# 32 bytes in front of the inner activations of two feed-forward layers: their start moves from 96 to 0 modulo 128

## The chip, the core and the metric

The kernel runs on one core of a Trainium2 chip. The metric is the device time of one execution in microseconds (us), as the median of several runs. Three runs of the kernel before took 557.93, 558.11 and 560.37 us.

## What is computed

Soft-capped attention over 2 batches of 12 heads (448 tokens, head size 64) is followed by two feed-forward layers on its 896 x 768 result. Each layer multiplies by a 768 x 2048 matrix, applies an activation, and multiplies by a 2048 x 768 matrix.

```python
def _attn_ref(q, k, v, cap):
    scores = scale * np.matmul(q, k.transpose(0, 1, 3, 2))
    scores = cap * np.tanh(scores / cap)
    scores = scores - np.max(scores, axis=-1, keepdims=True)
    attn = np.exp(scores)
    attn = attn / (np.sum(attn, axis=-1, keepdims=True) + 1e-09)
    return np.matmul(attn, v).astype(np.float32)

x = attn_out.transpose(0, 2, 1, 3).reshape(B * S, H * D)      # 896 x 768
h = x @ moe_w_in        # 768 x 2048
g = np.where(h >= 1, h, np.where(h <= -1, 0.0, (h + 1) ** 2 / 4))
x = g @ moe_w_out       # 2048 x 768
h = x @ moe2_w_in
g = np.maximum(0.01 * h, h)
out = g @ moe2_w_out
```

## The kernel before, in words

**Stages.** The attention runs in six steps of four heads each. Its result is kept transposed in SBUF as `xh` and `xl` (lines 178 and 179): the model's 768 columns lie in 6 chunks of 128 partitions, and the 896 tokens in the free dimension, as two batches of 448. Then follow four stages of matmuls: the first layer in (called in-stage 1 here), the first layer out (out-stage 1), the second layer in (in-stage 2), the second layer out (out-stage 2). An in-stage reads `xh` and `xl` and makes `gh` and `gl`, 16 chunks of 128 partitions by 896 tokens; an out-stage reads `gh` and `gl` and makes the next `xh` and `xl`, or the output.

**High and low parts.** Every float32 operand is split into a part that the reduced format fp32r holds and the rest: `xh` and `xl`, `gh` and `gl`, and for the weights `whi` and `wlo`. A product is made of three matmuls (`products`, lines 241 to 251): `whi` with the high part (line 247), `whi` with the low part (line 248), `wlo` with the high part (line 251). Each loads a 128 x 128 block of weights into the array, which the profile shows as PEld, and streams 448 columns of the activations, which are the moving operand. For a weight chunk the six matmuls come in the order 247, 248 for batch 0, 247, 248 for batch 1, then 251 twice. In-stages and out-stages go through the same six lines, with the same weight buffers.

**Weights.** They arrive as 64-bit numbers, are converted by ACT and DVE (`weights`, lines 194 to 239) and land in four pairs of buffers `whi0`/`wlo0` to `whi3`/`wlo3` (line 192), which all four stages use in turn. A block of weights is 768 columns wide in an in-stage and 512 in an out-stage. `Plan.order` sets one order of issue for all engines ahead of time.

**Where the tiles lie.** The tiles of a pool are laid out one behind the other, and each begins at a multiple of 32 bytes within a partition. The built program has these start addresses:

| tile | bytes per partition | start | start modulo 128 |
|---|---|---|---|
| `xh` | 21504 | 16512 | 0 |
| `xl` | 21504 | 38016 | 0 |
| `whi0` (first of the 8 weight buffers) | 3072 | 78048 | 96 |
| `wlo3` (last of them) | 3072 | 99552 | 96 |
| `gh` | 57344 | 102624 | 96 |
| `gl` | 57344 | 159968 | 96 |
| `a0`, `a1`, `a2` | 3584 each | 217312 on | 96 |

Three one-column tiles (`capb`, `rcap`, `half`) of 32 bytes each stand behind `xl`, which is why everything behind them lies at 96. All steps within these tiles (3584 bytes from chunk to chunk, 1792 from batch to batch, 512 from one 128-column block of weights to the next) are multiples of 128, so a tile's remainder is that of every matmul operand in it. `gh`, `gl` and the three `a` tiles, which hold the activation on its way from PSUM to `gh` and `gl`, are in the pool "layers" (lines 597 to 600). It opens when the first activation of a layer is issued, over the place of the attention's pool, which closes there.

Of the kernel before, what the change touches and what calls it, by code (L numbers as in the profile page):

```python
# [8 lines left out]
F32 = mybir.dt.float32  # L9
# [116 lines left out]
def tile_softcap_attention_ffn_ffn(  # L126
# [23 lines left out]
    NPAIR, P, _, S = qt.shape  # L150
# [443 lines left out]
    with tc.manual_schedule():  # L594
        for _, t in plan.order():
            if t["part"] == "act" and not later:
                st.close()
                pool = ctx.enter_context(tc.tile_pool(name="layers", bufs=1))
                later["g"] = [pool.tile([P, KF, NT], F32R, name=x) for x in ("gh", "gl")]
                later["a"] = [pool.tile([P, B, S], F32, name=f"a{n}") for n in range(3)]  # L600
            t["fn"]()
# [51 lines left out]
```

## Time and profile before

| | before |
|---|---|
| median of three runs | 558.11 us |
| the profiled execution | 558.62 us |
| its span from first to last instruction | 556.8 us |
| PE (matmuls) busy | 549.4 us, 99% of the span |
| PEld (weight loads) busy | 461.4 us, 83% |
| DVE busy | 394.4 us, 71% |
| ACT busy | 265.0 us, 48% |
| attention and its overlap with in-stage 1 | 0 to 91.4 us |
| in-stage 1, undivided part | 91.4 to 204.3 us |
| out-stage 1 | 204.3 to 321.0 us |
| in-stage 2 | 321.0 to 436.3 us |
| out-stage 2 | 436.3 to 552.8 us |

Each matmul's duration overlaps the next one's, and its end is modelled, so a busy share of 99% doesn't tell how fast the matmuls follow each other. That is read from their starts: start to start, in a stretch where the engine waits for nothing. The 1.8 us between the execution's time and its span lie before the first and after the last instruction.

### The profile page before, as it was taken

To read this page: it belongs to the slowest core of one execution; us is meant where nothing else is said; L and a number is where in the kernel's file an instruction comes from. 1 tells how busy PE (TensorE), PEld (TensorE's weight loads), DVE (VectorE), ACT (ScalarE), POOL (GpSimd) and SP (SyncE) were. 2 spreads that over 40 slices of the span, in tenths; PEclk is the share of its full clock that TensorE was granted. 3 is DMA by queue.
4 is the path that set the end of the run, shared out by engine and by line. 5 is a ranking of instruction groups with operands and counts; after the bars stand their busy time and mean duration, and the time that the engine had idled before them with its cause. 6 is when DMAs were issued, how large, how long until landed. Compare 5 with 4: busy or idle time off the path is not lost.

```text
span 556.8 us, 7429 instructions
## 1 busy us (share of the span) xinstructions
PE 549.4 (99%) x2935; PEld 461.4 (83%) x2935; DVE 394.4 (71%) x562; ACT 265.0 (48%) x314; POOL 1.4 (0%) x10
## 2 busy tenths in 40 slices
PE   7999999999999999999999999999999999999997
PEld 4233336999999999999999999999999999999996
DVE  1678787889999988665666579988877755546420
ACT  6999993086667563332223145544444332232210
POOL 0000000000000000000000000000000000000000
PEclk9999999999999999999999999999999999999999
DMA  8555633713332323333324524334222253543400
GB/s 225 163 152 169 199 87 76 215 54 117 114 114 97 112 77 114 114 102 126 105 90 145 171 69 157 116 114 160 86 77 76 52 154 93 150 143 98 125 34 33
DMA packets 25091, 65.06 MB, mean 117 GB/s; under 512 B 5856, under 2 KB 12000, under 8 KB 25056
## 3 DMA queue, kind: packets, MB, share of 16 engines
q1 hardware_dynamic: 24800, 64.24, 37.7%
q8 instruction: 23, 0.38, 0.3%
q10 hardware_dynamic: 224, 0.34, 0.3%
q14 instruction: 12, 0.10, 0.1%
q0 software_dynamic: 32, 0.00, 0.0%
HBM read 61.74 MB, written 2.80 MB: 116 GB/s over the span
## 4 chain that ended last, share of the span: by engine, by line
PE 97%; ACT 2%; issue 0%; DVE 0%
PE d L247 28%; PE d L251 28%; PE d L248 28%; PE d L360 5%; PE d L381 5%; PE d L412 2%; PE d L377 1%; PE d L356 1%; ACT e L365 1%; ACT e L368 1%; PE d L312 1%; ACT a L505 0%; DVE zero L309 0%; DVE half L314 0%
## 5 line engine op out<-in xcount | busy, mean ns | idle before, releaser
L247 PE MATMUL d<-gh,whi 128*128 128x448 f32 x384 | 140.2, 365 | 0.0
L248 PE MATMUL d<-gl,whi 128*128 128x448 f32 x384 | 140.2, 365 | 0.0
L247 PE MATMUL d<-xh,whi 128*128 128x448 f32 x384 | 139.5, 363 | 0.0
L248 PE MATMUL d<-xl,whi 128*128 128x448 f32 x384 | 139.2, 362 | 0.0
L238 ACT CAST whi<-w 128x512 fp32r<-128x512 f32 (+1 forms) x77 | 54.0, 701 | 146.2 <-PE d L248 96.7
L251 PE MATMUL d<-xh,wlo 128*128 128x448 f32 x384 | 111.9, 362 | 0.0
L251 PE MATMUL d<-gh,wlo 128*128 128x448 f32 x384 | 111.7, 365 | 0.0
L172 DVE TENSOR_TENSOR wlo<-w,whi 128x512 fp32r<-128x512 f32 (+1 forms) x80 | 63.5, 794 | 57.5 <-ACT whi L238 57.3
L247 PEld LDWEIGHTS d<-xh,whi 128*128 128x128 f32 x384 | 72.1, 188 | 6.9 <-issue 2.2
L247 PEld LDWEIGHTS d<-gh,whi 128*128 128x128 f32 x384 | 72.1, 188 | 5.7
L251 PEld LDWEIGHTS d<-gh,wlo 128*128 128x128 f32 x384 | 72.1, 188 | 5.7
L248 PEld LDWEIGHTS d<-gl,whi 128*128 128x128 f32 x384 | 72.1, 188 | 5.7
L251 PEld LDWEIGHTS d<-xh,wlo 128*128 128x128 f32 x384 | 72.1, 188 | 4.7
L248 PEld LDWEIGHTS d<-xl,whi 128*128 128x128 f32 x384 | 72.1, 188 | 4.7
L230 ACT ACTIVATE w<-wr 128x512 f32<-128x512 f32 (+1 forms) x77 | 58.5, 760 | 18.7 <-DMA wr<-w1i 8.8
L220 DVE SCALAR_TENSOR_TENSOR w<-wr,w 128x512 int32<-128x512 int32 (+1 forms) x80 | 63.8, 798 | 2.5
L216 DVE SCALAR_TENSOR_TENSOR w<-wr,w 128x512 int32<-128x512 int32 (+1 forms) x80 | 63.8, 798 | 2.4
L471 DVE TENSOR_TENSOR a<-d,a 128x896 f32<-128x896 f32 x32 | 34.7, 1087 | 16.2 <-ACT a L470 15.7
L365 ACT ACTIVATE e<-d,rcap 128x896 f32<-128x896 f32 x42 | 39.6, 1002 | 6.5 <-PE d L360 6.0
L208 DVE TENSOR_SCALAR w<-w 128x512 f32<-128x512 f32 (+1 forms) x80 | 37.9, 473 | 3.8 <-ACT w L230 3.6
L212 DVE TENSOR_SCALAR w<-w 128x512 int32<-128x512 int32 (+1 forms) x80 | 38.4, 480 | 2.7
L368 ACT ACTIVATE e<-e,capb 128x1792 f32<-128x1792 f32 (+1 forms) x18 | 36.7, 2038 | 0.5
(47 smaller groups left out, 320.3 us busy)
## 6 DMA issues: line engine op xcount, KB each, us to landing
wr<-w1o SPq DMA_DIRECT2D x24, 512.0 KB, 3.6
wr<-w2i SPq DMA_DIRECT2D x16, 768.0 KB, 4.3
wr<-w2o SPq DMA_DIRECT2D x24, 512.0 KB, 3.7
wr<-w1i SPq DMA_DIRECT2D x11, 768.0 KB, 4.3
wr<-w1i SPq DMA_DIRECT2D x15, 256.0 KB, 4.9
bc<-rr SPq DMA_DIRECT2D x12, 224.0 KB, 3.9
out<-a SPq DMA_DIRECT2D x12, 224.0 KB, 4.3
v<-vt SPq DMA_DIRECT2D x5, 512.0 KB, 4.6
```

The lines of the kernel that those rows point to most:

```text
L172: nc.vector.tensor_tensor(out=out_, in0=x, in1=f32(hi), op=ALU.subtract)
L208: nc.vector.tensor_scalar(out=f32(w), in0=f32(w), scalar1=W_MIN, scalar2=W_MAX, op0=ALU.max, op1=ALU.min)
L212: nc.vector.tensor_scalar(out=w, in0=w, scalar1=3, scalar2=LOW_30, op0=ALU.logical_shift_left, op1=ALU.bitwise_and)
L216: nc.vector.scalar_tensor_tensor(out=w, in0=r[:, :, 1], scalar=SIGN_AND_TOP, in1=w, op0=ALU.bitwise_and, op1=ALU.bitwise_or)
L220: nc.vector.scalar_tensor_tensor(out=w, in0=r[:, :, 0], scalar=29, in1=w, op0=ALU.logical_shift_right, op1=ALU.bitwise_or)
L230: add("ACT", act(n) + 0.06, lambda: nc.scalar.activation(f32(w), f32(r[:, :, 1]), AF.Abs), R, [W])
L238: add("ACT", act(n), lambda: nc.scalar.copy(h, f32(w)), [W], [H])
L247: nc.tensor.matmul(o[:, b, :S], ch, h[:, f, r], start=first, stop=False)
L248: nc.tensor.matmul(o[:, b, :S], ch, l[:, f, r], start=False, stop=False)
L251: nc.tensor.matmul(o[:, b, :S], cl, h[:, f, r], start=False, stop=last)
L365: add("ACT", act(2 * S, 1), lambda: nc.scalar.activation(e, d[:, :, :S], AF.Tanh, scale=rcap), [("d", s)], [key(j, g)])
L368: lambda: nc.scalar.activation(whole, whole, AF.Exp, scale=capb), [], [key(j, g)])
```

## The change

A tile of 8 float32 per partition (32 bytes) is taken from the pool "layers" ahead of the others. Nothing writes or reads it. `gh` then starts at 102656, `gl` at 160000 and `a0` at 217344, all multiples of 128. The weights, `xh` and `xl` stay where they were, and the last tile ends at 228096. Every engine's instructions stand in the same order as before, with waits on the same engines at the same places.

```diff
             if t["part"] == "act" and not later:
                 st.close()
                 pool = ctx.enter_context(tc.tile_pool(name="layers", bufs=1))
+
+                pool.tile([P, 8], F32, name="pad")
                 later["g"] = [pool.tile([P, KF, NT], F32R, name=x) for x in ("gh", "gl")]
                 later["a"] = [pool.tile([P, B, S], F32, name=f"a{n}") for n in range(3)]
             t["fn"]()
```

## Rows read from the trace of the kernel before

**Rows 1.** The page: engines' busy time, and the granted TensorE clock in 40 slices.
```profile
PE 549.4 (99%) x2935; PEld 461.4 (83%) x2935; DVE 394.4 (71%) x562; ACT 265.0 (48%) x314; POOL 1.4 (0%) x10
PEclk9999999999999999999999999999999999999999
```

**Rows 2.** All waits of PE: engine, line waited for, us in total, times, longest.
```profile
PE d L381 <- ACT e L368: 2.4, 2, 1.4
PE d L312 <- DVE half L314: 1.4, 1, 1.4
```

**Rows 3.** PE's groups by form: line, operands, count, busy us, mean ns, idle before.
```profile
L247 PE MATMUL d<-gh,whi 128*128 128x448 f32 x384 | 140.2, 365 | 0.0
L248 PE MATMUL d<-gl,whi 128*128 128x448 f32 x384 | 140.2, 365 | 0.0
L247 PE MATMUL d<-xh,whi 128*128 128x448 f32 x384 | 139.5, 363 | 0.0
L248 PE MATMUL d<-xl,whi 128*128 128x448 f32 x384 | 139.2, 362 | 0.0
```

**Rows 4.** Timeline, PE, in-stage 2: start us, duration, line, matmul (x2: two merged).
```profile
379.86 0.36 PE L247 MATMUL d<-xh,whi 128*128 128x448 f32 x1
380.06 0.36 PE L248 MATMUL d<-xl,whi 128*128 128x448 f32 x1
...
384.66 0.36 PE L247 MATMUL d<-xh,whi 128*128 128x448 f32 x1
```

**Rows 5.** The same view: the edges of out-stage 1.
```profile
204.29 0.36 PE L247 MATMUL d<-gh,whi 128*128 128x448 f32 x1
...
321.03 0.37 PE L247 MATMUL d<-xh,whi 128*128 128x448 f32 x1
321.23 0.36 PE L248 MATMUL d<-xl,whi 128*128 128x448 f32 x1
321.44 0.37 PE L247 MATMUL d<-xh,whi 128*128 128x448 f32 x1
321.64 0.37 PE L248 MATMUL d<-xl,whi 128*128 128x448 f32 x1
321.85 0.57 PE L251 MATMUL d<-xh,wlo 128*128 128x448 f32 x2
322.26 0.36 PE L247 MATMUL d<-xh,whi 128*128 128x448 f32 x1
```

**Rows 6.** The same view, all engines: first matmul of out-stage 2, and the kernel's end.
```profile
436.26 0.36 PE L247 MATMUL d<-gh,whi 128*128 128x448 f32 x1
...
552.79 0.37 PE L251 MATMUL d<-gh,wlo 128*128 128x448 f32 x1
553.20 0.53 ACT L505 COPY a<-d 128x448 f32<-128x448 f32 x1 [1.90 <-PE d L251]
553.75 0.33 SPq L506 DMA_DIRECT2D out<-a  x1
```

**Rows 7.** Line 251: operation, count: duration in ns, min/median/max, first and last start.
```profile
L251 PE MATMUL d<-xh,wlo x384: 360/362/370, 85.8 to 436.1; 128*128 128x448 f32 x192
L251 PE MATMUL d<-gh,wlo x384: 362/365/369, 205.1 to 552.8; 128*128 128x448 f32 x192
```

**Rows 8.** Busy us of each engine (count) in four stretches: the in- and out-stages in turn.
```profile
92.00:204.00 112.00, 112.00 (x562) 105.12 (x561) 103.37 (x137) 63.86 (x76) 0.00 (x0) 1.00 0.35 110
204.00:320.80 116.80, 116.80 (x578) 108.27 (x577) 77.37 (x125) 35.52 (x54) 0.00 (x0) 1.00 0.38 120
320.80:436.20 115.40, 115.40 (x578) 108.26 (x578) 95.48 (x120) 54.65 (x66) 0.00 (x0) 1.00 0.32 104
436.20:552.90 116.70, 116.70 (x578) 108.06 (x576) 56.93 (x99) 31.77 (x53) 0.00 (x0) 1.00 0.34 103
```

**Rows 9.** All waits, longest in total: the first row.
```profile
ACT whi L238 <- PE d L248: 96.7, 32, 4.2
```

## The prediction

> **What bounds the kernel now.** I read the page's busy shares first. PE is busy 99% of the span, and its clock is granted in full throughout, so the level is 2.4 GHz from the first slice to the last [rows 1]. Next come the waits: PE waits twice for ACT and once for DVE, 3.8 us in all, and every one of these lines (381, 312) is in the attention or ahead of it [rows 2]. From the first feed-forward matmul to the last, PE waits for nobody. The four feed-forward stages fill 461 of 556.8 us, and their time is the number of matmuls times the interval from one start to the next. Only that interval can move the end; nothing that DVE, ACT or the DMA queues gain reaches it.
>
> So the third view is the timeline, read by starts. In in-stage 2 the matmul of line 247 starts at 379.86 and, 24 matmuls (four weight chunks of six) later, again at 384.66: 4.80 us / 24 = 200.0 ns each [rows 4]. The out-stages run slower. Out-stage 1 has 24 blocks of 4 chunks of 6 matmuls, 576 in all; its first starts at 204.29 and the first of the next stage at 321.03: 116.74 us / 576 = 202.67 ns [rows 5]. Out-stage 2 has 575 intervals from 436.26 to 552.79: 116.53 us / 575 = 202.66 ns [rows 6]. The reader is to see a constant surplus of 2.67 ns, and that it isn't noise: the groups by form show it too, 365 ns for the two of `gh` and `gl` against 363 and 362 for those of `xh` and `xl` [rows 3], and the medians of line 251 are 365 and 362 [rows 7].
>
> This is an experiment that the kernel before makes by itself. An out-stage matmul and an in-stage matmul come from the same three lines, have the same shape, load 128 x 128 weights from the same eight buffers (all at 96 modulo 128) and write the same PSUM tiles in turn. What differs is where the moving operand lies: `xh` and `xl` begin at 0 modulo 128, `gh` and `gl` at 96, as the weights do. The load on the other engines doesn't explain it, since it is the other way round: DVE is busy 103.4 of 112 us and 95.5 of 115.4 in the in-stages, and 77.4 of 116.8 and 56.9 of 116.7 in the out-stages [rows 8]. The out-stages differ by 20 us of DVE work and agree in the interval within 0.01 ns.
>
> **The change, part by part.** The pad itself issues nothing: no instruction, wait or transfer is added, and none changes its place. The three things that move by 32 bytes are `gh`, `gl` and the `a` tiles.
>
> *Moving operand of the out-stages.* After the change `gh` and `gl` lie against the weights, modulo 128, as `xh` and `xl` do today. I take today's in-stage interval for them. Out-stage 1: 576 x 200.0 = 115.20 instead of 116.74, a gain of 1.54 us. Out-stage 2: 575 x 200.0 = 115.00 instead of 116.53, 1.53 us. All of it lies on the path that sets the end, as PE has no wait in these stages to give it back to.
>
> *The slow start of in-stage 2.* The first six intervals after the switch from `gh` to `xh` take 322.26 - 321.03 = 1.23 us, 205 ns each, before 200 is reached [rows 5]. I read this as the out-stage's rhythm running out. If the out-stage runs as the in-stage, it goes, worth 0.03 us.
>
> *Bounds of the interval.* The shortest duration of line 251 with `xh` is 360 ns against a median of 362 [rows 7], so an estimate of the lower end is 198 ns: 1151 x 2 = 2.3 us more gain. The upper end of what is still a gain is today's 202.67, none at all. I take 200.0, since it is the value of hundreds of matmuls with the same remainders.
>
> *Writes of ACT and DVE to `gh`, `gl` and `a`, and the output DMAs from `a`.* They could get faster or slower, but nothing waits for them on PE. Their cover is the stock of converted weights and activations: ACT's largest wait is for PE to free a weight buffer, 96.7 us in 32 waits [rows 9], so the weights are ready early, and in the out-stages DVE has over 39 us idle in each [rows 8]. A stage 1.5 us shorter doesn't use that up. Only the last copy and DMA behind the last matmul are uncovered, 553.20 on [rows 6]; the copy takes 0.53 us, and I cost its change at nothing, bounds 0.1 us either way as a fifth of it.
>
> *Sum.* 1.54 + 1.53 + 0.03 = 3.10 us. The profiled execution's 558.62 us becomes 555.5, its span 553.7. It stands 0.5 us above the median of 558.11; with the same gain the median becomes 555.0 us, 0.56% less.
>
> **The rivals.** *The address isn't the cause, or not modulo 128.* Something else in an out-stage makes the 2.67 ns: blocks 512 instead of 768 columns wide, or an effect that repeats at 256 bytes. Modulo 256, `xh` and `xl` lie at 128, the weights at 224, `gh` and `gl` at 224 before and at 0 after. So the after-case is not the in-stage's case in that bit, and no row shows it. Bit 8 at least is cleared: the two batches of one chunk are 1792 bytes apart, which flips it from matmul to matmul, and the in-stage keeps 200.0 for both [rows 4]. Time by this rival: 558.1 us. Against it speaks that the interval follows the operand and nothing else that I can name.
> The rule that the Trainium skill gives supports this rival: by "SBUF — State Buffer", section "Who interferes with whom", PE has two independent read ports, one for the moving operand and one for LDWEIGHTS, and never waits on anyone. By that rule the weights' address can't matter to the stream, the 32 bytes would do nothing, and the sum would be zero. The trace doesn't agree in the simple form, as rows with the same work differ by 2.67 ns; it leaves open whether a meeting of the two reads or the moving operand's own start is behind it, and both give the forecast here.
>
> *Half the effect.* If the stream's own start and its place against the weights each cost something, one could stay: half of 3.1 us, 556.6.
>
> *Slower: the two reads meet more often.* The moving operand will begin 32 bytes behind the weights modulo 256, in place of level with them; in the in-stages it is 160 behind. If a bank's turn makes 32 bytes worse than level, every out-stage matmul would take what the slowest do today: 369 ns against 365 in line 251 [rows 7], 4 ns more. 1151 x 4 = 4.6 us, 562.7. It decides from 2.4 ns more per matmul on (1151 x 2.4 = 2.8 us, half a per cent). For it: rows as slow exist, 205 ns after the stage switch [rows 5]. Against it: these are passing, and the settled in-stage has the same 32 modulo 64 and 128.
>
> *More than forecast.* 198 ns as above: 552.7 us.
>
> **How the numbers follow.** Half a per cent, about what a measurement of this kernel can tell from no change, is 2.8 us: faster means below 555.3. The forecast (interval within half a ns of 200, so 554.4 to 555.6 us) gets 0.77, no effect 0.13, half 0.04, slower 0.04, more 0.02. The forecast's centre lies only 0.3 us below the border; I give 0.7 of its chance to the near side: 0.54, with the 0.02 of more, 0.56 for faster. Same takes 0.23 + 0.13 + 0.04 = 0.40, slower 0.04. The forecast's own range holds less than 8 in 10, so the range reaches up to no effect and its spread: 554.2 to 558.5 us.
>
> **What the profile after would show.** Right: starts 24 matmuls apart differ by 4.80 us in the out-stages as in the in-stages; durations of the `gh` and `gl` groups fall from 365 to 362 or 363; the out-stages take 115.2 and 115.0 us; the attention and in-stage 1 keep their times; in-stage 2 loses its slow first six matmuls; PE still waits only in lines 381 and 312. Wrong: out-stage intervals still at 202.67 (address not the cause), above 203 (the reads meet), or 200.0 intervals with new PE waits for `whi` or `gh` (the supply has become late).

## The result

| | before | after |
|---|---|---|
| median of five runs each | 558.28 us | 566.41 us (562.28 to 568.5) |
| ratio, with its 95% interval | | 1.0118 [1.0083, 1.0153] |
| the profiled execution | 558.62 us | 566.41 us |
| its span | 556.8 us | 564.6 us |

The change makes the kernel slower by 0.8 to 1.5%; 555.0 us had been forecast. In the experiments, single runs of several layouts, the kernel before among them, lie near 570 us and apart from the rest; ratios leave them out, and their count is told.

The profile after, in the views of [rows 1, 3, 2]: the page's busy times, PE's groups by form (mean ns of one behind the busy us), and PE's waits.

```profile
PE 557.2 (99%) x2935; PEld 459.7 (81%) x2935; DVE 394.5 (70%) x562; ACT 264.3 (47%) x314; POOL 1.3 (0%) x10
```
```profile
L247 PE MATMUL d<-xh,whi 128*128 128x448 f32 x384 | 141.3, 368 | 0.0
L247 PE MATMUL d<-gh,whi 128*128 128x448 f32 x384 | 141.0, 367 | 0.0
L248 PE MATMUL d<-xl,whi 128*128 128x448 f32 x384 | 141.0, 367 | 0.0
L248 PE MATMUL d<-gl,whi 128*128 128x448 f32 x384 | 140.1, 365 | 0.0
```
```profile
PE d L381 <- ACT e L368: 2.3, 2, 1.4
PE d L312 <- DVE half L314: 1.4, 1, 1.4
```

PE is still busy throughout and waits in the same two lines, so the time went into the intervals between matmuls. The surprise stands in the first and third row of groups: `xh` and `xl`, which did not move, went from 363 and 362 ns to 368 and 367, and are now the slower ones. The timeline of PE and PEld in in-stage 1 shows where that begins (start us, duration, engine, line):

```profile
104.86 0.36 PE L248 MATMUL d<-xl,whi 128*128 128x448 f32 x1
...
109.06 0.36 PE L248 MATMUL d<-xl,whi 128*128 128x448 f32 x1
...
109.66 0.19 PEld L248 LDWEIGHTS d<-xl,whi 128*128 128x128 f32 x1 [0.21 <-DVE xl L172]
109.66 0.47 PE L248 MATMUL d<-xl,whi 128*128 128x448 f32 x1
...
109.97 0.36 PE L251 MATMUL d<-xh,wlo 128*128 128x448 f32 x1
...
110.17 0.37 PE L247 MATMUL d<-xh,whi 128*128 128x448 f32 x1
```

Up to 109.06 the interval is 4.20 us / 21 = 200.0 ns. At 109.66 the weight load for a matmul on the last head pair's `xl` comes 0.2 us late, as `xl` is only just written; one interval takes 0.31 us. From 110.17 to the first matmul of out-stage 1, 465 matmuls later, it is (206.27 - 110.17) / 465 = 206.67 ns, and it never goes back within the stage. In the execution before, the same weight load came at the last moment too; the write of `xl` by DVE and the load, before:

```profile
109.58 1.09 DVE L172 TENSOR_TENSOR xl<-xf,xh 128x896 fp32r<-128x896 f32 x1
...
110.72 0.19 PEld L248 LDWEIGHTS d<-xl,whi 128*128 128x128 f32 x1
```

and the write of `xl` after:

```profile
108.51 1.09 DVE L172 TENSOR_TENSOR xl<-xf,xh 128x896 fp32r<-128x896 f32 x1
```

Before, `xl` was written at 110.67 us, 0.05 us ahead of the load; after, at 109.60, when the load had been due at 109.46. Counted from the start of in-stage 1, DVE began this write 18.20 us in before and 18.37 us in after. The edges of the later stages, after:

```profile
206.27 0.37 PE L247 MATMUL d<-gh,whi 128*128 128x448 f32 x1
...
324.03 0.37 PE L247 MATMUL d<-xh,whi 128*128 128x448 f32 x1
...
443.06 0.37 PE L247 MATMUL d<-gh,whi 128*128 128x448 f32 x1
...
560.61 0.37 PE L251 MATMUL d<-gh,wlo 128*128 128x448 f32 x1
```

Against [rows 5, 6]: the out-stages take 117.76 and 117.55 us instead of 116.74 and 116.53 (204.4 ns for 202.7), in-stage 2 takes 119.03 instead of 115.23 (206.7 for 200.0). In-stage 1 begins 1.23 us earlier in this execution (at 90.14 instead of 91.38 us, by the attention's start) and takes 3.22 us more. Sum: -1.23 + 3.22 + 1.02 + 3.80 + 1.02 = 7.83 us, the whole difference of the spans. The granted clock is 1.00 in all of these stretches.

So one matmul stream, with the same operands at the same addresses, ran at 200.0 ns before a short wait and at 206.67 behind it. That made theory H: the interval is a rhythm that PE carries on from matmul to matmul. The layout fixes which rhythms exist, and a wait, an odd matmul or a shift of the moving operand at a stage switch can throw PE from one into another. The rival W: addresses alone fix the interval, among them those to which ACT and DVE write `gh`, `gl` and `a`.

### The profile page after: what moved, and what is told of

Its sections match the earlier page's. It is cut to its first block, busy times and chain, and to the rows that moved or that the text cites. A ratio compares the mean times of both kernels' runs of the same rounds, so it can differ in the third digit from the quotient of the medians.

```text
span 564.6 us, 7429 instructions
## 1 busy us (share of the span) xinstructions
PE 557.2 (99%) x2935; PEld 459.7 (81%) x2935; DVE 394.5 (70%) x562; ACT 264.3 (47%) x314; POOL 1.3 (0%) x10
## 4 chain that ended last, share of the span: by engine, by line
PE 98%; ACT 2%; issue 0%; DVE 0%
PE d L247 28%; PE d L251 28%; PE d L248 28%; PE d L381 5%; PE d L360 5%; PE d L412 2%; PE d L377 1%; PE d L356 1%; ACT e L365 1%; ACT e L368 1%; PE d L312 1%; ACT a L505 0%; DVE zero L309 0%; DVE half L314 0%
## 5 line engine op out<-in xcount | busy, mean ns | idle before, releaser
L247 PE MATMUL d<-xh,whi 128*128 128x448 f32 x384 | 141.3, 368 | 0.0
L248 PE MATMUL d<-xl,whi 128*128 128x448 f32 x384 | 141.0, 367 | 0.0
L251 PE MATMUL d<-xh,wlo 128*128 128x448 f32 x384 | 113.8, 367 | 0.0
L470 ACT ACTIVATE a<-d 128x896 f32<-128x896 f32 x16 | 14.7, 918 | 49.2 <-PE d L251 49.2
```

Of the source, the lines that this page charges most:

```text
L247: nc.tensor.matmul(o[:, b, :S], ch, h[:, f, r], start=first, stop=False)
L248: nc.tensor.matmul(o[:, b, :S], ch, l[:, f, r], start=False, stop=False)
L251: nc.tensor.matmul(o[:, b, :S], cl, h[:, f, r], start=False, stop=last)
```

## The experiments

All stages' means below are worked out from the starts in the timeline, as above.

### The wait taken away, and a wait put in

The first kernel is the changed one with some matmuls done again ahead of the last `xl`:

```diff
         for b in bs:
             r = slice(b * S, (b + 1) * S)
+            for _ in range(5 if first and g == 1 and b == 0 else 0):
+                nc.tensor.matmul(o[:, b, :S], ch, h[:, f, r], start=True, stop=True)
             nc.tensor.matmul(o[:, b, :S], ch, h[:, f, r], start=first, stop=False)
```

> The changed kernel, with the first matmul of the second weight block's batch 0 done six times instead of once (five extra matmuls, about 1.0 us), so that PE reaches the last head's xl later and doesn't wait for it at 109.7 us. Theory H (the interval is a state that PE carries on; a wait of 0.1 us throws in-stage 1 from 200.0 to 206.7 ns and nothing brings it back): no wait, in-stage 1 stays at 200.0 ns to its end, and the later stages start from the fast state, so in-stage 2 has a chance of 200.0 again; out-stages at 200.0 to 204.5. Span 555 to 558 us with the extra 1.0 us. Rival W (the addresses alone decide, among them those to which ACT and DVE write gh, gl and a): in-stage 1 goes to 206.7 ns without any wait, in-stage 2 and the out-stages stay at 206.7 and 204.5; span about 565 us.

Five runs took 563.87 to 568.9 us (ratio to the kernel before 1.0090 [1.0051, 1.0128], the extra matmuls included); the profiled span was 564.1 us. Without a wait in it, in-stage 1 kept 200.0 ns to its end. Its groups by form and stage edges:

```profile
L249 PE MATMUL d<-gh,whi 128*128 128x448 f32 x384 | 141.7, 369 | 0.0
L249 PE MATMUL d<-xh,whi 128*128 128x448 f32 x384 | 139.5, 363 | 0.0
```
```profile
207.08 0.36 PE L249 MATMUL d<-gh,whi 128*128 128x448 f32 x1
...
326.11 0.37 PE L249 MATMUL d<-xh,whi 128*128 128x448 f32 x1
...
441.32 0.36 PE L249 MATMUL d<-gh,whi 128*128 128x448 f32 x1
...
560.14 0.37 PE L253 MATMUL d<-gh,wlo 128*128 128x448 f32 x1
```

The out-stages took (326.11 - 207.08) / 576 = 206.65 ns and 118.82 / 575 = 206.64, and in-stage 2 between them 115.21 / 576 = 200.0. W falls: the writes go where they go with the change, and both in-stages are at 200.0. H's first half holds, but its hope for the out-stages (200.0 to 204.5) was wrong: entered from 200.0 they run at 206.65, entered from 206.67 at 204.44. Both are worse than 202.67. So the change costs 1151 x 4.0 ns = 4.6 us even where nothing waits, and 3.22 + 1.02 + 3.80 + 1.02 = 9.1 us with the wait. The five runs of the changed kernel, 4.0 to 10.2 us above 558.28, span both, but only one of them was profiled.

The second kernel is the one before with a later `xl`:

```diff
-        add("DVE", vec2(n), lambda: nc.vector.tensor_copy(hi, xf), [("xf", y)], H)
+        def high():
+            for _ in range(2 if j == NQ - 1 else 1):
+                nc.vector.tensor_copy(hi, xf)
+
+        add("DVE", vec2(n), high, [("xf", y)], H)
```

> The kernel before, with the last head pair's copy to xh done twice (0.65 us of DVE), so that its xl is written late and PE waits for it once in in-stage 1. Theory H: PE waits about 0.4 us at 110 us; behind it in-stage 1 runs at about 206.7 ns instead of 200.0, for some 470 matmuls or 3.1 us; out-stage 1 goes back to 202.7, in-stage 2 to 200.0; span 556.8 + 0.4 + 3.1 = 560.3 us. Rival W (addresses alone): in-stage 1 stays at 200.0 after the wait; span 557.2 us.

The profiled span was 558.2 us. PE waited behind the matmuls at 110.4 and 111.0 us: these two intervals are 0.35 and 0.93 us longer than 0.20. From 112.41 on the matmuls ran at 200.0 ns again, to the stage's end:

```profile
112.11 0.47 PE L248 MATMUL d<-xl,whi 128*128 128x448 f32 x1 [0.66 <-DVE xl L172]
...
112.61 0.36 PE L247 MATMUL d<-xh,whi 128*128 128x448 f32 x1
112.81 0.36 PE L248 MATMUL d<-xl,whi 128*128 128x448 f32 x1
```

My expectation of 206.7 ns was wrong in this execution: a wait can throw the rhythm, it need not. By itself the run decides nothing between H and W. Of ten runs eight took 558.6 to 561.5 us (ratio 0.9995 [0.9975, 1.0015]), two 570.6 and 571.4.

### The rhythm pushed on purpose

A matmul of another length ahead of each accumulation disturbs the stream without any wait. Its sum is overwritten by the next matmul (`kicks` is a counter that starts at 0).

```diff
         for b in bs:
             r = slice(b * S, (b + 1) * S)
+            if first and b == bs[0]:
+                kicks[0] += 1
+                m = 64 * (1 + kicks[0] % 6)
+                nc.tensor.matmul(o[:, b, :m], ch, h[:, f, r.start:r.start + m], start=True, stop=True)
             nc.tensor.matmul(o[:, b, :S], ch, h[:, f, r], start=first, stop=False)
```

> The changed kernel, with an extra matmul of 64, 128, 192, 256, 320 or 384 columns in turn ahead of each accumulation's first matmul (some 50 in all, 0.2 us each, 10 us), each a disturbance of PE's rhythm. Theory H: the interval that holds between two disturbances takes more than one value within the same stage, at the same addresses (200.0 and 206.7 ns in the in-stages), and changes only at a disturbance. Rival W (addresses alone): one interval for each stage, whatever the disturbance, after a few matmuls.

The timeline of PE around an extra matmul of 256 columns and the next one, of 320, in in-stage 2:

```profile
414.00 0.36 PE L253 MATMUL d<-xh,whi 128*128 128x448 f32 x1
...
415.20 0.28 PE L252 MATMUL d<-xh,whi 128*128 128x256 f32 x1
...
416.55 0.37 PE L253 MATMUL d<-xh,whi 128*128 128x448 f32 x1
...
421.51 0.37 PE L253 MATMUL d<-xh,whi 128*128 128x448 f32 x1
...
422.75 0.31 PE L252 MATMUL d<-xh,whi 128*128 128x320 f32 x1
...
424.10 0.36 PE L253 MATMUL d<-xh,whi 128*128 128x448 f32 x1
...
428.90 0.36 PE L253 MATMUL d<-xh,whi 128*128 128x448 f32 x1
```

Six matmuls take 1.20 us up to the first extra one (200.0 ns). Behind it 24 take 421.51 - 416.55 = 4.96 us (206.7), and behind the second 428.90 - 424.10 = 4.80 us (200.0). Within the in-stages 256 columns pushed the stream from 200.0 to 206.7 five times out of five, and 320 columns brought it back each time; no other length did either. A sixth matmul of 256 columns, right at the switch from out-stage 1 to in-stage 2, found the stream at 206.7 and left it at 200.0, so the length alone doesn't fix what follows. In the out-stages, with `gh` at 0 modulo 128 throughout, three rhythms followed each other: 200.0 behind 4 of the 13 extra matmuls, 206.7 behind 8, 204.4 behind one. A stretch of out-stage 1, behind 64 columns:

```profile
268.26 0.36 PE L253 MATMUL d<-gh,whi 128*128 128x448 f32 x1
...
285.86 0.36 PE L253 MATMUL d<-gh,whi 128*128 128x448 f32 x1
```

It holds 88 matmuls, 17.60 us / 88 = 200.0 ns. The changed address isn't slow in itself; the rhythm is, into which the stream falls.

> The kernel before with an extra matmul of 64, 128, 192, 256, 320 or 384 columns in turn ahead of each accumulation's first matmul. Theory H: the in-stages show 200.0 ns, and 206.7 ns after an extra 256 columns, as in the changed kernel with the same extra matmuls, since xh and xl lie where they did; the out-stages show 202.7 and at least one other interval. Rival W: out-stages at 202.7 ns throughout, as their addresses are the same as before.

With the layout of before the in-stages answered the same lengths in the same way, 206.7 five times out of five behind 256 and 200.0 behind the sixth at the switch. The out-stages hardly answered at all: 202.7 ns behind 12 of 13. A stretch behind the same 64 columns as above:

```profile
267.84 0.36 PE L253 MATMUL d<-gh,whi 128*128 128x448 f32 x1
...
282.43 0.36 PE L253 MATMUL d<-gh,whi 128*128 128x448 f32 x1
```

These are 72 matmuls, 14.59 us / 72 = 202.6 ns. Only behind the last extra matmul, where the last output chunk's batches are computed one after the other, did the stream run at 206.67 to the end; without extra matmuls the same chunk ran at 202.67. So where moving operand and weights are level modulo 128 (the same remainder), the stream fell back into one middling rhythm in 12 cases of 13, and a second one exists. The change took the middling one away.

### The shift at the stage switch, or the place against the weights

```diff
-                pool.tile([P, 8], F32, name="pad")
+                pool.tile([P, 40], F32, name="pad")
```

> The change with a pad of 160 bytes instead of 32: gh, gl and a start at 0 modulo 128 as with the change, but at 128 modulo 256, as xh and xl do. If the out-stages' interval follows the start modulo 256 (rival: bit 7 of the address), they run at the in-stages' own interval of that run, 200.0 or 206.7 ns; if modulo 128 is all, they run at 204.5 ns with the pattern of the changed kernel (205, 206, 202). In-stage 1 by theory H is 200.0 or 206.7 according to whether PE waited in it.

555.39 us, with all of `gh` and `gl` at 362 ns:

```profile
L248 PE MATMUL d<-gl,whi 128*128 128x448 f32 x384 | 139.2, 362 | 0.0
L247 PE MATMUL d<-gh,whi 128*128 128x448 f32 x384 | 139.2, 362 | 0.0
```

Both out-stages and in-stage 2 ran at 200.00 ns, although PE had waited 0.5 us at 110 us. This is close to the forecast's 555.0 us, from another pad. It may mean that the out-stages want 128 modulo 256, or that the switch from `xh` to `gh` no longer shifts the stream and so no longer pushes it. The next kernel tells these apart: it moves the weights by 128 bytes instead (and with them the buffers in which weights are converted and the attention's tiles), so that all moving operands stay level with each other while their place against the weights is that of `gh` in the changed kernel.

```diff
     half = const.tile([P, 1], F32, name="half")
+    const.tile([P, 32], F32, name="wpad")
```

> 128 bytes in front of the weight buffers, and the change's 32 in front of gh: xh, xl, gh and gl all begin at 128 modulo 256, and the weights at 96 modulo 256 instead of 224. The moving operand then stands against the weights as gh does in the changed kernel (32 bytes above them, modulo 256), but it doesn't shift at a stage switch. If the place against the weights makes the slow intervals: 204.4 or 206.7 ns in the stages, span about 565 us. If the shift of the moving operand at the switch does: 200.0 ns in all four stages unless a wait breaks it, span about 554 us.

572.87 us, which neither side had expected. The timeline of PE has the answer in it:

```profile
103.64 0.36 PE L248 MATMUL d<-xh,whi 128*128 128x448 f32 x1
...
111.44 0.36 PE L248 MATMUL d<-xh,whi 128*128 128x448 f32 x1
...
112.41 0.47 PE L248 MATMUL d<-xh,whi 128*128 128x448 f32 x1 [0.20 <-DVE xh L434]
113.53 0.47 PE L249 MATMUL d<-xl,whi 128*128 128x448 f32 x1 [0.66 <-DVE xl L172]
...
114.66 0.37 PE L248 MATMUL d<-xh,whi 128*128 128x448 f32 x1
...
115.90 0.37 PE L248 MATMUL d<-xh,whi 128*128 128x448 f32 x1
```

Up to the wait, 39 matmuls take 7.80 us: 200.0 ns, at the very place against the weights that the rival called slow. Behind it six take 1.24 us, 206.7 ns, and the three later stages ran at 206.67, 206.66 and 206.67 ns. Without a shift at the switches the rhythm is carried through them, the good one with the 160-byte pad and the bad one here. The place against the weights, in the rival's form, falls. No run has all moving operands at 0 modulo 256, so it isn't shown whether the shift itself pushes the stream, or the start at 0 that it leads to.

> The 160-byte pad alone, timed. Theory H: the wait for the last xl is still there in some runs and can end in the 206.7 ns rhythm, which would then hold through all stages, since nothing shifts it: most runs near 555 us, some near 555 + 2180 x 6.67 ns = 569.5 us. Rival (bit 7 of the address alone decides): every run near 555 us, whatever the wait.

Seven runs with the 160-byte pad: 554.40 to 557.17 us in six, 569.89 in one; ratio 0.9917 [0.9882, 0.9951]. As H had it: faster, but not safe. The run of 569.89 wasn't profiled; it has the time that H gives a run thrown into 206.7 ns.

### Taking the wait away for good

> The 160-byte pad (gh at 128 modulo 256, level with xh), and in in-stage 1 the fourth weight block's first four chunks of batch 1 are done ahead of the last head pair's chunks instead of behind them, which gives the last xl 2.4 us more before PE needs it. Theory H with the switch (the rhythm is carried over a stage switch unchanged where the moving operand's start is the same modulo 256, and only a wait breaks it): no wait in in-stage 1, all four stages at 200.0 ns in every run, 555.4 less the 0.5 us of waiting seen with the 160-byte pad, 554.9 us, with a spread under 1.5 us from the attention's start alone. Rival (160 bytes was one lucky run): times scattered between 555 and 570 as with the other layouts.

Twelve runs took 555.65 to 559.04 us, ratio 0.9951 [0.9932, 0.9970], none near 570; the profile has all stages at 200.0 ns. But the wait had only moved: the fifth block now waited for a PSUM bank, 1.1 us in PE's waits, as the first gate (line 471) came later.

```profile
PE d L247 <- DVE a L471: 1.1, 1, 1.1
```

> The 160-byte pad, and two chunks (1.2 us) instead of four of the fourth block's batch 1 done ahead of the last head pair's chunks. Theory H: the wait for the last xl shrinks or goes, and no wait for a PSUM bank takes its place, as its gate has 4.8 us; all stages at 200.0 ns; median 554.5 to 555.3 us. Rival (the order of the blocks makes a new wait, as with four chunks): 556 to 557 us.

Of 13 runs six took 554.5 to 557.7 us and seven 569.7 to 572.3. The profiled one is of the seven, with a granted clock of 1.00 in every stage. The wait for `xl` had gone, and a short one for the same gate stood in its place (timeline of PE's weight loads, first row), behind which all stages ran at 206.67 ns and the groups show 367 and 368 ns:

```profile
119.97 0.19 PEld L247 LDWEIGHTS d<-xh,whi 128*128 128x128 f32 x1 [0.32 <-DVE a L471]
```
```profile
L247 PE MATMUL d<-xh,whi 128*128 128x448 f32 x384 | 141.3, 368 | 0.0
L247 PE MATMUL d<-gh,whi 128*128 128x448 f32 x384 | 141.1, 367 | 0.0
```

Both expectations of 554 to 555 us were wrong. Both ways of reordering traded one wait for another, and with the 160-byte pad one short wait can cost 14 us (some 2160 intervals, 6.67 ns more each).

### A distance with one rhythm

The remaining distances between moving operand and weights, in steps of 32 bytes modulo 128, were tried with the extra matmuls; all moving operands at 128 modulo 256.

> xh, xl, gh, gl at 128 modulo 256 and the weights at 32 modulo 256 (the moving operand 96 above them, modulo 128), with the extra matmuls of 64 to 384 columns ahead of each accumulation. If two rhythms are there wherever moving operand and weights are not level modulo 128: 200.0 ns between most extra matmuls, and 206.7 behind some, which one fixed by the extra columns. If the distance decides which rhythms exist: a different set, for instance one interval alone.

> The same with the weights at 64 modulo 256, 64 bytes from the moving operand modulo 128, the only distance in steps of 32 that no other run has. Two rhythms, 200.0 and 206.7 ns, if every layout that isn't level has both; another set, or one interval alone, if the distance decides.

| weights mod 256 | moving operand mod 256 | distance mod 128 | intervals seen, ns | kernels |
|---|---|---|---|---|
| 224 | 128 (in-stages) | 32 | 200.0 and 206.7 | before, changed |
| 224 | 0 (out-stages) | 32 | 200.0, 204.4, 206.7 | changed |
| 96 | 128 | 32 | 200.0 and 206.7 | weights moved by 128 |
| 224 | 224 (out-stages) | 0 | 202.7 (206.7 once, at the end) | before |
| 32 | 128 | 96 | 205.3 to 205.4 only | weights at 32 |
| 64 | 128 | 64 | 200.0 only | weights at 64 |

The last two rows as the timeline of PE has them: a stretch of out-stage 1 with the weights at 32, behind 64 columns, and one of in-stage 2 with the weights at 64, behind 256 columns.

```profile
272.75 0.37 PE L254 MATMUL d<-gh,whi 128*128 128x448 f32 x1
...
290.00 0.37 PE L254 MATMUL d<-gh,whi 128*128 128x448 f32 x1
```
```profile
413.44 0.28 PE L253 MATMUL d<-xh,whi 128*128 128x256 f32 x1
...
413.97 0.36 PE L254 MATMUL d<-xh,whi 128*128 128x448 f32 x1
...
418.77 0.36 PE L254 MATMUL d<-xh,whi 128*128 128x448 f32 x1
```

The first is 17.25 us / 84 = 205.4 ns, the second 4.80 us / 24 = 200.0. Neither start alone decides: with the weights at 224 the moving operand at 224 has another set of intervals than at 128 or 0, and with the moving operand at 128 weights at 224, 32 and 64 have three sets. The distance modulo 128 sorts the rows, up to the 204.4 of the second. That it is the rule is argued, as the distances 0, 64 and 96 were each seen in one layout only. At 64 bytes none of the 49 extra matmuls, of any length, in any stage, moved the stream off 200 ns. The last kernel is that layout without extra matmuls (against the changed one):

```diff
     half = const.tile([P, 1], F32, name="half")
+    const.tile([P, 24], F32, name="wpad")
...
-                pool.tile([P, 8], F32, name="pad")
+                pool.tile([P, 16], F32, name="pad")
```

> No extra matmuls: 96 bytes in front of the weight buffers (they begin at 64 modulo 256) and 64 in front of gh (xh, xl, gh, gl at 128 modulo 256), the order of the work as before. If the distance of 64 bytes has the 200 ns rhythm alone: 200.0 ns in all four stages in every run, whatever PE waits for in in-stage 1; 554 to 558 us, no run near 570, and a ratio to the kernel before of 0.991 to 0.995. Theory H without that (every layout can be thrown into 206.7 ns): some runs of 566 to 572 us, as with the 160-byte pad.

Median 556.42 us of twelve runs, 554.51 to 558.72, none near 570; ratio 0.9929 [0.9908, 0.9950]. PE waited for `xl` and kept its rhythm:

```profile
PE d L249 <- DVE xl L172: 0.4, 1, 0.4
```
```profile
207.03 0.36 PE L248 MATMUL d<-gh,whi 128*128 128x448 f32 x1
...
552.43 0.37 PE L252 MATMUL d<-gh,wlo 128*128 128x448 f32 x1
```

From the first matmul of out-stage 1 to the last of the kernel, 1727 intervals take 345.40 us: 200.0 ns. The kernel beats the one before by 0.7% and, by the two ratios (0.9929 / 1.0118), the changed one by 1.9%. It has the only layout with all stages at 200 ns that the runs didn't find a way to spoil.

## Why the prediction was wrong, point by point

- **What bounds the kernel: right.** Only PE's interval moved the end. The sum over the stages gives the whole difference; DVE, ACT and the queues are nowhere in it.
- **The moving operand of the out-stages: the step that failed.** "I take today's in-stage interval for them", since it is "the value of hundreds of matmuls with the same remainders". The 200.0 ns were not a property of the remainders modulo 128 but of a rhythm that the in-stages had fallen into. The term of -3.07 us measured +2.04 us in the profiled execution, and +4.6 us where PE entered the out-stages undisturbed. With the 160-byte pad, where the stream isn't shifted at the switch, the same term came to -3.07 us, with 1151 intervals of 200.0.
- **Bit 7 of the address.** The prediction named it as what no row showed, gave it 0.13 and priced it at no effect. That it could turn out worse than 202.67 was left out: an unknown bit has a price on both sides.
- **The slow start of in-stage 2: the hint that was there.** "I read this as the out-stage's rhythm running out": intervals of 205 ns with `xh` at 0 modulo 128 [rows 5] showed that one address has more than one interval, and that PE remembers. It was priced at 0.03 us and not followed.
- **"The attention and in-stage 1 keep their times": wrong.** The last `xl` was finished 0.05 us before its weight load in the execution before, with nothing to spare; in the one after it was 0.17 us later against in-stage 1's start, behind a DMA that DVE waits for in both executions, and came too late. Against the run without a wait, the wait of 0.1 us cost 3.2 us in in-stage 1 and 3.8 in in-stage 2, and gave back 2.5 us in the out-stages (204.44 for 206.65). Whether such a wait costs the layout of before more than in-stage 1 isn't shown: its out-stages came back to 202.7 behind nearly all extra matmuls, but no profile has one entered from 206.7.
- **Slower, "the two reads meet more often": right in sign, and its 562.7 us is close to the lowest run of 562.28.** Its 4 ns are also what the out-stages showed without a wait (206.65 for 202.67). But that it came out so is luck: by its mechanism the place of 32 bytes above the weights costs every matmul the same, and at this place the stream also ran at 200.0.
- **The rule of two read ports.** The Trainium skill ("SBUF — State Buffer", section "Who interferes with whom") has PE's two reads independent, and by that rule their places against each other would not matter. The runs don't agree: with the moving operands where they were and the same stream of matmuls, moving the weights by 32 bytes, from 64 to 32 modulo 256, took the interval from 200.0 to 205.3 ns. The buffers in which weights are converted and the attention's tiles moved along, but no matmul of these stages reads them.

What stays open: why the distances of 0, 32, 64 and 96 have these rhythms, which of them a wait ends in (at the same place in in-stage 1 some waits left 200.0 and some 206.7), and whether the kernel before's runs from 570 us on (8 of the 67 beside the experiments) are in-stages and out-stages in the 206.7 ns rhythm, which would be some 12 us (2291 intervals, a half at +6.7 and a half at +4.0). None of those was profiled, and two of them, 573.4 and 576.1 us, lie higher than that.

## What to carry to other kernels

In a stream of back-to-back matmuls with a weight load each, check the start-to-start interval stage by stage; if it has more than one value for the same work, the start addresses of weights and activations are worth a few runs. Don't carry an interval over from another stage because the addresses agree: disturb the stream (an odd matmul now and then) and see whether it comes back to the same interval, and take a layout that does. A layout that has the best interval and a worse one beside it is a gamble that a wait of 0.1 us can lose.

## What the runs showed of the hardware that was not expected

A matmul stream without any wait has several steady intervals at one clock (granted 1.00, so 2.4 GHz) and one layout, and remembers which for over a thousand matmuls, through changes of stage where the moving operands are level modulo 256. All of them fit one grid of 13.33 ns, 32 cycles of that clock, an estimate worked out from the intervals: 200.0 is 15 of it, two of 206.67 are 31, three of 204.44 are 46, five of 202.67 are 76, five of 205.33 are 77. At 202.67, 204.44 and 205.33 the recorded starts repeat after just that many matmuls, five, three and five. At 206.67 they show no such alternation (the intervals are 206 to 208 ns in turn), and with the weights at 64 the 200.0 repeats after three (201, 198, 201), so the grid explains these two only in part. That weight load and stream meet on such a grid is argued from these numbers, not shown.
